# Seven products for the last two token chunks of layer one's first gMLP half

## The chip, the cores and the metric

The kernel runs on one core of a Trainium2 chip. The metric is the device time of one execution, in microseconds (us). A core has five engines with queues of their own: TensorE (PE in the profile; its weight loads are PEld) multiplies, VectorE (DVE) and GpSimd (POOL) do elementwise work, ScalarE (ACT) applies functions and copies, SyncE (SP) starts DMA transfers. GpSimd starts some transfers too. Each engine works through its queue in the order in which the program recorded it, and waits on semaphores for the others.

## The reference

Two layers, each a linear attention block and then a gated MLP, on 2048 tokens of 512 features, all in float32. Each block adds its result to x. The second half of the MLP is normalised and mixed over the tokens by a 2048 x 2048 matrix.

```python
def _B_ref(x, w_in, w_sp, b_sp, w_out):
    z = _gelu(jnp.einsum("bsd,df->bsf", x, w_in))
    z1 = z[..., :Fh]
    z2 = _layernorm(z[..., Fh:], axis=-1)
    g = jnp.einsum("ts,bsf->btf", w_sp, z2) + b_sp[None, :, None]
    return jnp.einsum("bsf,fd->bsd", z1 * g, w_out)
...
x = A_x
x = x + _A_ref(_layernorm(x, axis=-1), A_wqkv, A_wo)
x = x + _B_ref(_layernorm(x, axis=-1), B_w_in, B_w_sp, B_b_sp, B_w_out)
x = x + _A_ref(_layernorm(x, axis=-1), A_wqkv, A_wo)
x = x + _B_ref(_layernorm(x, axis=-1), B_w_in, B_w_sp, B_b_sp, B_w_out)
```

w_in is 512 x 1792, Fh is 896.

## The kernel before

A float32 product is made of three matmuls in a faster type: each operand is split into a high part (`high`, a copy by ScalarE) and a low part (`low`, a subtraction by VectorE), and high x high, low x high and high x low are added up in a PSUM bank (`mm3`, L228 to L230). Tokens go in 16 tiles of 128 (`NT`), or four chunks of 512 (`NCHK`); Fh is seven feature blocks of 128 (`NF`).

The class `P2` is the stage of a layer that ends the attention and makes both halves of the MLP's first product. `run` is layer one's loop over steps s = 1 to 18. In step s, one after another: `b` splits the turned attention result of tile s; `c` multiplies tile s - 1 by the output weights (12 matmuls of 512 columns); `c2` adds it to x and takes the statistics; `c3` normalises the tile (ScalarE) and writes it to memory, from where it is read back to be turned by VectorE (`Turn`: stores by L419, loads by L196, the turn L448); `d` splits the turned tile s - 2 into the operands `xT` of its chunk; `e4` normalises the MLP's second half of tile s - 4 with a mean and a scale (`zms`); `e` multiplies tile s - 3 by the second half's weights (two banks of 448 columns, 24 matmuls), `e2` puts both through gelu, `e3` takes the statistics of the 896 columns, by VectorE in layer one; and twice `f` makes one feature block of the first half, transposed, for a whole chunk (12 matmuls of 512), with gelu and a store (`fout`) behind. So an f can only be made once the four tiles of its chunk are there. The seven f's that are left after step 18, all of chunk 3, are made at the head of the spatial stage (`P4.run`, the loop `while p2.f()`).

Layer two makes the first six features of chunks 2 and 3 otherwise. The features f and f + 3, the two chunks and the two halves of the 512 inner features make 2 x 2 blocks, and seven products of such blocks do for eight: each is 6 matmuls, and sums and differences of blocks are their operands. `first_a` and `first_b` are products 1 and 2, into the bank u, with a copy of u after product 1 into a second bank y; `T1`, `T1split`, `T2` and `raw` make the operands by VectorE and ScalarE; `tail` makes products 5, 6, 7, 3 and 4 and the sums of the results. The weights' sums are made by `FSums` from win1 and kept in memory (`w1sums`): in layer two's first stage, three pairs f by f, with the additions on GpSimd.

Beside this stage run `sums` (sums and differences of blocks of the spatial weights, four additions on GpSimd for two `tick`s, loads and stores by SyncE) and, in steps 9 to 15, the stores of the split weights win1 for layer two (`w1parts`, two a step, `WSTORE`). The last `LEFT` ticks are left to the spatial stage, which is a list of steps g: 14 of the product P2 (12 matmuls of 512 columns each), then P1 with 24 each, and so on (L1922 to L1924).

The order of all queues is that of these calls as written; small tables (`WSTORE`, `WADD`, `LEFT`, `FILL`) say in which step a piece is recorded. Tiles are taken from lists of SBUF pages (pg), quads (qd), bigs (bg), and PSUM banks.

## Time and profile before

| what | value |
|---|---|
| median of 3 runs | 1345.61 us (1345.12 to 1345.69) |
| profiled execution, its own time | 1345.32 us |
| its span | 1343.5 us |
| TensorE busy, share | 1338.9 us, 100% |
| VectorE, ScalarE, GpSimd busy | 1042.9, 726.6, 460.2 us |
| granted TensorE clock | 1.0 |
| layer one's e(11) to the spatial stage | 282.31 to 350.30 us |

The page's groups give line, engine, operation, tiles (out <- in), shape, busy time, mean, and idle time before; the timeline gives start and length of single instructions; lines with SPq or POOL and DMA are the issues of transfers. A matmul's recorded length overlaps its neighbours', so the time from start to start is the one that counts.

### The profile page before, as it was taken

What the parts mean: (1) busy time and instruction counts of PE and PEld (TensorE: products, weight loads), DVE (VectorE), ACT (ScalarE), POOL (GpSimd) and SP (SyncE); (2) the same over time, 40 slices, a digit from 0 to 9 for tenths busy, and PEclk for the clock granted to TensorE, in tenths of its full rate; (3) what the DMA queues carried; (4) which work ended last, traced back from release to release, by engine and by line L of the source; (5) the groups of instructions that cost most, each with busy time, mean ns of one, the idle gap of its engine ahead of it and who ended that gap; (6) DMA issues with size and microseconds to landing.
All of it is one profiled execution on the core that took longest, in us unless ns stands there. A gap on an engine that the chain in (4) does not pass through costs nothing.

```text
span 1343.5 us, 19219 instructions
## 1 busy us (share of the span) xinstructions
PE 1338.9 (100%) x6547; PEld 1142.0 (85%) x6547; DVE 1042.9 (78%) x1662; ACT 726.6 (54%) x1219; POOL 460.2 (34%) x613
## 2 busy tenths in 40 slices
PE   9999999999999999999999999999999999999999
PEld 7888888888888888889988888888888888888898
DVE  7779877753797699898867878777679858899885
ACT  5764634334642265445677755557687433666454
POOL 3755765534122400301425443544531012122021
PEclk9999999999999999999999999999999999999999
DMA  5898477878977986894777662678767545579344
GB/s 184 284 313 282 158 256 250 284 254 270 316 234 256 289 267 203 282 320 80 174 169 235 167 142 84 202 243 259 229 211 234 170 164 176 178 245 312 123 79 64
DMA packets 172403, 290.30 MB, mean 216 GB/s; under 512 B 14480, under 2 KB 53904, under 8 KB 172048
## 3 DMA queue, kind: packets, MB, share of 16 engines
q1 hardware_dynamic: 154048, 251.45, 56.5%
q0 software_dynamic: 18112, 37.49, 13.4%
q8 instruction: 51, 0.84, 0.3%
q14 instruction: 48, 0.39, 0.1%
q10 hardware_dynamic: 144, 0.13, 0.0%
HBM read 204.08 MB, written 101.71 MB: 228 GB/s over the span
## 4 chain that ended last, share of the span: by engine, by line
PE 98%; DVE 1%; DMA 0%; ACT 0%; POOL 0%; issue 0%; SPq 0%; POOLq 0%
PE bank L230 14%; PE bank L228 14%; PE bank L229 14%; PE bank L1922 12%; PE bank L1923 12%; PE bank L1924 12%; PE bank L2120 3%; PE bank L2121 3%; PE bank L2122 3%; PE bank L988 1%; PE bank L989 1%; PE bank L990 1%; PE bank L384 1%; PE bank L1155 1%; PE bank L1157 1%; PE bank L1156 1%
## 5 line engine op out<-in xcount | busy, mean ns | idle before, releaser
L1923 PE MATMUL bank<-qd,pg 128*128 128x512 f32 x736 | 286.4, 389 | 0.0
L1922 PE MATMUL bank<-qd,pg 128*128 128x512 f32 x736 | 286.3, 389 | 0.0
L1924 PE MATMUL bank<-qd,pg 128*128 128x512 f32 x736 | 286.3, 389 | 0.0
L1697 ACT ACTIVATE qd<-qd 128x1024 fp32r<-128x1024 f32 x142 | 149.5, 1053 | 128.2 <-PE bank L1924 108.0
L1700 DVE TENSOR_TENSOR qd<-qd,qd 128x1024 fp32r<-128x1024 f32 x132 | 167.8, 1274 | 54.1 <-ACT qd L1697 54.1
L230 PE MATMUL bank<-qd,pg 128*128 128x512 f32 x448 | 174.7, 390 | 0.0
L1924 PEld LDWEIGHTS bank<-qd,pg 128*128 128x128 f32 x736 | 138.2, 188 | 28.8
L1923 PEld LDWEIGHTS bank<-qd,pg 128*128 128x128 f32 x736 | 138.2, 188 | 28.6
L1922 PEld LDWEIGHTS bank<-qd,pg 128*128 128x128 f32 x736 | 138.2, 188 | 28.6
L1963 POOL TENSOR_TENSOR bg<-bg,pg 128x512 f32<-128x512 f32 x28 | 46.9, 1676 | 217.9 <-ACT qd L1697 100.3
L228 PE MATMUL bank<-qd,pg 128*128 128x512 f32 x308 | 120.2, 390 | 0.2 <-ACT pg L214 0.2
L229 PE MATMUL bank<-qd,pg 128*128 128x512 f32 x308 | 120.0, 390 | 0.0
L230 PEld LDWEIGHTS bank<-qd,pg 128*128 128x128 f32 x448 | 84.1, 188 | 18.2 <-DVE pg L217 0.4
L363 POOL TENSOR_SCALAR rs<-mv 128x1 f32<-128x1 f32 x80 | 24.7, 308 | 191.3 <-DVE mv L361 186.9
L214 ACT ACTIVATE pg<-pg 128x512 fp32r<-128x512 f32 x85 | 53.0, 624 | 64.6 <-DVE pg L448 21.3
L372 ACT ACTIVATE pg<-pg,nb,rs 128x512 f32<-128x512 f32 x52 | 42.1, 812 | 84.5 <-POOL nb L366 79.0
L1606 POOL TENSOR_TENSOR pg<-pg,pg 128x512 f32<-128x512 f32 x48 | 67.2, 1400 | 58.2 <-DVE pg L1762 52.1
L2122 PE MATMUL bank<-wo,qd 128*128 128x256 f32 x288 | 81.5, 283 | 0.0
L2120 PE MATMUL bank<-wo,qd 128*128 128x256 f32 x276 | 78.1, 283 | 0.0
L2121 PE MATMUL bank<-wo,qd 128*128 128x256 f32 x276 | 78.0, 283 | 0.0
L229 PEld LDWEIGHTS bank<-qd,pg 128*128 128x128 f32 x308 | 57.8, 188 | 12.1 <-DVE qd L217 0.3
L228 PEld LDWEIGHTS bank<-qd,pg 128*128 128x128 f32 x308 | 57.8, 188 | 12.1 <-ACT pg L214 0.4
(278 smaller groups left out, 3280.4 us busy)
## 6 DMA issues: line engine op xcount, KB each, us to landing
qd<-s SPq DMA_DIRECT2D x62, 512.0 KB, 4.4
qd<-in_wsp_dram SPq DMA_DIRECT2D x40, 512.0 KB, 4.1
qd<-hP SPq DMA_DIRECT2D x40, 512.0 KB, 4.7
pg<-z SPq DMA_DIRECT2D x56, 256.0 KB, 4.7
pg<-in_wsp_dram SPq DMA_DIRECT2D x52, 256.0 KB, 4.3
s<-pg SPq DMA_DIRECT2D x48, 256.0 KB, 3.8
z<-pg SPq DMA_DIRECT2D x40, 256.0 KB, 3.3
pg<-w POOLq DMA_DIRECT2D x38, 256.0 KB, 4.7
```

Of the source, the lines that this page charges most:

```text
L228: nc.tensor.matmul(out, ah, bh, start=start, stop=False)
L229: nc.tensor.matmul(out, ah, bl, start=False, stop=False)
L230: nc.tensor.matmul(out, al, bh, start=False, stop=stop)
L1606: nc.gpsimd.tensor_tensor(t, a, b, op=OP.add)
L1697: self.mark = nc.scalar.activation(w[:, 0], r, AF.Copy)
L1700: nc.vector.tensor_sub(w[:, 1], r, w[:, 0].bitcast(F32))
L1922: m(out, h[:, o], w[:, 0, j, :], start=start, stop=False, skip_group_check=True)
L1923: m(out, h[:, o], w[:, 1, j, :], start=False, stop=False, skip_group_check=True)
L1924: m(out, l[:, o], w[:, 0, j, :], start=False, stop=stop, skip_group_check=True)
L2120: m(out, A, x, start=start and f == 0, stop=False, skip_group_check=True)
L2121: m(out, A, y, start=False, stop=False, skip_group_check=True)
L2122: m(out, B, x, start=False, stop=stop and f == 2, skip_group_check=True)
```

## The change

Layer one gets the seven products for features 0 to 5 of chunks 2 and 3. `run` records no f of chunk 3 but the seventh, `FONE` says how many f's a step has, product 1 of pair s - 15 stands at the head of steps 15, 16 and 17 with its copy, product 2 at their ends, and `tail` now serves both layers at the head of the spatial stage. Tile 15 is turned by TensorE (four transposes) rather than through memory. The statistics of tiles 10 to 15 are ScalarE's: the gelu's accumulated sum, a square with a sum, and GpSimd's small operations. The weights' sums are loaded, added (now VectorE), split and stored in steps 13 to 18. The w1parts stores move from steps 9 to 15 to steps 4 to 10. Ten ticks of the spatial sums, not four, are left to the spatial stage, from g = 13 on, their loads fetched at g = 12 rather than 14. Turned tiles above 4 lie in the z tiles.

```diff
-WSTORE = 9
+WSTORE = 4
...
-WADD = {2: 0, 4: 1, 6: 2}
+FONE = {6: 2, 7: 2, 8: 2, 9: 1, 10: 2, 11: 2, 12: 2, 13: 1, 14: 1}
+WADD = {13: 0, 14: 1, 15: 2}
...
-LEFT = 4
+LEFT = 10
+TLAST = 13
+TFIRST = 13
+ACTFROM = 10
...
+            self.raw, self.kept, self.made = {}, deque(), []
...
-                nc.gpsimd.tensor_tensor(o, a, b, op=op)
+            self.raw[f] = [load(win1_d[f + 3 * k]) for k in range(2)]
...
+            raw = self.raw.pop(f)
+            p, q = (t.rearrange("p (k n) -> p k n", k=2) for t in raw)
+            V = nc.vector
+            V.tensor_add(q[:, 1], q[:, 0], q[:, 1])
+            V.tensor_sub(q[:, 0], p[:, 0], q[:, 0])
+            V.tensor_sub(p[:, 0], q[:, 1], p[:, 0])
+            V.tensor_sub(p[:, 1], p[:, 1], p[:, 0])
...
+                h, l = pages.get(PAGE, F32R), pages.get(PAGE, F32R)
...
+                self.made.append((f, m, h, l))
+            pages.put(*raw)
+        def store(self):
+            for f, m, *t in self.made:
...
+                    nc.sync.dma_start(w1sums[f, m][k], t[k].bitcast(F32))
+                if m:
+                    pages.put(*t)
+                else:
+                    self.kept.append(t)
+            self.made = []
...
-            self.wf = deque([w1parts[f] for f in list(range(NF)) * 2 + [0, 6, 1, 2, 6]]
+            self.wf = deque([] if not L else [w1parts[f] for f in list(range(NF)) * 2 + [0, 6, 1, 2, 6]]
...
-            self.qturn, self.xturn = Turn(f"qt{L}", range(5), True), Turn(f"yt{L}", (0, 1, 2, 3, NT - 1) if L else range(4), home=ZHome if L else None)
+            self.qturn, self.xturn = Turn(f"qt{L}", range(5), True), Turn(f"yt{L}", (0, 1, 2, 3, NT - 1), home=ZHome, copy=bool(L))
...
+        def by_act(self, i):
+            return self.L or i >= ACTFROM
...
-                more = {"accum_out": self.acc(i)[:, j:j + 1]} if self.L else {}
+                more = {"accum_out": self.acc(i)[:, j:j + 1]} if self.by_act(i) else {}
...
-            if not self.L:
+            if not self.by_act(i):
...
-                w = self.A[f] = self.ws.popleft()
+                w = self.A[f] = self.ws.popleft() if self.L else self.held1(f)
...
-                pages.put(*w)
+                if self.L:
+                    pages.put(*w)
+        def held1(self, f):
+            return [t[:, f].rearrange("p c n -> p (c n)") for t in (self.win1.h, self.win1.l)]
...
-                if f:
+                if f and self.L:
...
+        def tsplit(self, r):
+            if r not in self.T:
+                self.T6q = quads.get([P, 2, 2, 512], F32R)
+                self.T[r] = self.T6q[:, 0], self.T6q[:, 1]
+            t = self.t2 if r == 6 else self.b22
+            for k in range(2):
+                high(self.T[r][0][:, k], t[k])
+            for k in range(2):
+                low(self.T[r][1][:, k], t[k], self.T[r][0][:, k])
...
-            big = [bigs.get([P, NF, 512], F32R if k < 2 else F32) for k in range(3)]
-            c = [big[2][:, f] for f in range(3)]
-            room = Rooms(big[2][:, f] for f in range(3, NF))
+            L = self.L
+            big = [bigs.get([P, NF, 512], F32R if k < 2 else F32) for k in range(3 if L else 2)]
+            if L:
+                c = [big[2][:, f] for f in range(3)]
+                room = Rooms(big[2][:, f] for f in range(3, NF))
+            else:
+                c = [pages.get(PAGE) for _ in range(3)]
+                room = pages
...
-            self.T |= {6: (two(0, 0), two(0, 1)), 7: (two(0, 2), two(1, 0)), 4: (two(1, 1), two(1, 2))}
+            self.T |= {7: (two(0, 2), two(1, 0)), 4: (two(1, 1), two(1, 2))}
+            if L:
+                self.T[6] = two(0, 0), two(0, 1)
+                self.tsplit(6)
+            self.tsplit(7)
...
-            for r, t in ((6, self.t2), (7, self.b22)):
-                for k in range(2):
-                    high(self.T[r][0][:, k], t[k])
-                for k in range(2):
-                    low(self.T[r][1][:, k], t[k], self.T[r][0][:, k])
...
-            self.p4.loadb()
+            if L:
+                self.p4.loadb()
...
-                if f == 0:
+                if L and f == 0:
...
-                if f == 1:
+                if L and f == 1:
...
-            self.e3(NT - 2)
-            self.e3(NT - 1)
-            self.e4(NT - 4)
-            self.e4(NT - 3)
+            if not L:
+                quads.put(self.T6q)
+            if L:
+                self.e3(NT - 2)
+                self.e3(NT - 1)
+                self.e4(NT - 4)
+                self.e4(NT - 3)
...
-            for i in (NT - 2, NT - 1):
+            for i in (NT - 2, NT - 1) if L else ():
...
-                w = self.ws.popleft()
+                w = self.ws.popleft() if L else [t[:, 256:512] for t in self.held1(f + 3)]
...
-                pages.put(*w)
+                if L:
+                    pages.put(*w)
+            if not L:
+                self.win1.free()
...
+            if not L:
+                pages.put(*c)
...
                 return
             w1 = self.win1
             for s in range(1, NT + 3):
-                if s == NT + 2:
-                    sums.tick()
+                if s in (15, 16, 17):
+                    self.first_a(s - 15)
                 self.loadx(s + 1)
                 self.qturn.load(s + 1)
                 if s in self.qturn.by_pe:
...
+                if s == NT + 1:
+                    self.T1()
+                    self.T1split()
+                    self.T2()
+                if s == NT + 2:
+                    self.ws.extend(self.fsums.kept)
+                    quads.put(*self.xT.pop(2))
+                    self.tsplit(6)
+                    for _ in range(3):
+                        self.wfetch()
...
                     self.e(s - 3)
                     self.e2(s - 3)
                     self.e3(s - 3)
-                self.f()
-                self.f()
+                for _ in range(FONE.get(s, 0)):
+                    self.f()
+                if s in (15, 16, 17):
+                    self.first_b(s - 15)
+                    self.first_out(s - 15)
+                if s - 2 in WADD:
+                    self.fsums.store()
+                if s in WADD:
+                    if not WADD[s]:
+                        self.fsums = FSums()
+                    self.fsums.load(WADD[s])
+                if s - 1 in WADD:
+                    self.fsums.split(WADD[s - 1])
+                if s == NT:
+                    self.B = quads.get([P, 2, 2, 512])
+                    self.raw(0)
+                    self.raw(1)
+                    self.wf.extend(w1sums[f, 1] for f in range(3))
                 self.fq.extend(self.fnext)
                 self.fnext = []
                 w1.piece(True)
                 w1.fetch()
                 if self.L == 0:
-                    if s > 4:
-                        sums.tick(s < NT + 2)
+                    if s == TLAST + 1:
+                        sums.store()
+                    if 4 < s <= TLAST:
+                        sums.tick(s < TLAST)
                     if s >= WSTORE and s < WSTORE + NF:
                         for k, t in enumerate((w1.h, w1.l)):
                             nc.sync.dma_start(w1parts[s - WSTORE][k],
                                               t[:, s - WSTORE].rearrange("p c n -> p (c n)").bitcast(F32))
-                if s >= NT + 1:
-                    self.p4.fetch(s - NT - 1)
+                if s == NT + 2:
+                    self.p4.fetch(1)
             self.e4(NT - 1)
             self.win2.free()
...
-            if not early:
-                self.fetch(3)
-                self.sp(0)
-                self.fetch(4)
...
-            if not early:
-                self.zahead(1)
...
-            if early:
-                for _ in p2.tail():
-                    n += 1
-                    self.zahead(n - 1)
-                    self.sp(n - 1)
-                    if n < 3:
-                        self.fetch(n + 3)
-                self.zahead(3)
-            while p2.f():
-                self.zahead(min(self.zmade, 3))
+            for _ in p2.tail():
...
-                if n == SPN:
-                    self.sp(1)
-                    self.fetch(5)
+                self.zahead(n - 1)
+                self.sp(n - 1)
+                if n < 3:
+                    self.fetch(n + 3)
...
-            if p2.win1 is not None:
-                p2.win1.free()
...
-                if not early and g == 14:
+                if not early and g == TFIRST - 1:
...
-                if not early and 15 <= g <= 15 + LEFT:
+                if not early and TFIRST <= g <= TFIRST + LEFT:
...
```

The order, at three places. First ScalarE in the last two steps of the loop and behind it, before: gelus (L1070), outputs (L1137), normalise (L372), then the first split of the spatial stage.

```order
L1070 ACTIVATE z14_z0_3637<-bank5_136_3611 128x448
L1070 ACTIVATE z14_z0_3637<-bank6_137_3624 128x448
L1137 ACTIVATE pg6_368_3663<-bank4_138_3650 128x512
L372 ACTIVATE z14_z0_3637<-z14_z0_3637,nb_3648,rs_3645 128x896
L1070 ACTIVATE z15_z0_3712<-bank7_139_3686 128x448
L1070 ACTIVATE z15_z0_3712<-bank1_140_3699 128x448
L1137 ACTIVATE pg11_373_3738<-bank3_141_3725 128x512
L1137 ACTIVATE pg14_374_3755<-bank0_142_3742 128x512
L372 ACTIVATE z15_z0_3712<-z15_z0_3712,nb_3723,rs_3720 128x896
L1697 ACTIVATE qd4_20_3768<-qd1_18_3677 128x1024
```

And now, from e4(14) on: gelus (L1074), square (L1091), e4(15), two splits for product 7 (L218), the copies of product 5 (L1258), f's output (L1141) and the first copies of product 6 (L1274) into the banks of product 7.

```order
L376 ACTIVATE z14_z0_3648<-z14_z0_3648,acc_3649 128x896
L1074 ACTIVATE z15_z0_3716,acc_3717<-bank4_140_3690 128x448
L1074 ACTIVATE z15_z0_3716,acc_3717<-bank7_141_3703 128x448
L1091 ACTIVATE pg15_356_3721,acc_3717<-z15_z0_3716,acc_3717 128x896
L376 ACTIVATE z15_z0_3716<-z15_z0_3716,acc_3717 128x896
L218 ACTIVATE bg2_7_3730<-pg2_344_3609 128x512
L218 ACTIVATE bg2_7_3730<-pg13_345_3610 128x512
L1258 ACTIVATE pg8_357_3732<-bank5_143_3754 128x512
L1258 ACTIVATE pg6_358_3733<-bank6_144_3762 128x512
L1258 ACTIVATE pg14_359_3734<-bank4_145_3770 128x512
L1141 ACTIVATE pg20_360_3778<-bank2_142_3741 128x512
L1274 ACTIVATE bank5_146_3788<-bank3_125_3359 128x512
```

Between a tile's gelus and its e4 stands the square now, and the two splits and three copies stand behind e4(15).

GpSimd at the same place, now: the last three operations of tile 14 (L1100 to L1102), a store of an output, six loads of the weights' sums (L209), and tile 15's mean (L1081) with its three.

```order
L1100 TENSOR_SCALAR acc<-acc 128x1
L1101 TENSOR_TENSOR acc<-acc,mhalf 128x1
L1102 TENSOR_SCALAR acc<-acc 128x1
L1151 DMA z_0_2_2_3666<-pg_349_3664 128x512
L209 DMA pg_350_3677<-w1s_1_0_111 128x512
L209 DMA pg_351_3679<-w1s_1_1_112 128x512
L209 DMA pg_352_3681<-w1s_1_0_115 128x512
L209 DMA pg_353_3683<-w1s_1_1_116 128x512
L209 DMA pg_354_3685<-w1s_1_0_119 128x512
L209 DMA pg_355_3687<-w1s_1_1_120 128x512
L1081 TENSOR_SCALAR acc<-acc 128x1
```

Before, additions of the spatial sums (L1606) stood between the small operations of two tiles; now seven transfers stand between those of the last two.

VectorE ahead of product 5's operand, only now: the last lows of the weights' sums (L221), the two raw sums of chunk 2 (L1166), the low part of tile 15, and the operand (L1200, L1201, and its low part, L221). Of these, only low(15) stood there before.

```order
L221 TENSOR_TENSOR pg21_341_3574<-pg15_332_3459,pg0_340_3573 128x256
L221 TENSOR_TENSOR pg7_343_3580<-pg8_333_3461,pg20_342_3579 128x256
L221 TENSOR_TENSOR pg7_343_3580<-pg15_332_3459,pg20_342_3579 128x256
L1166 TENSOR_TENSOR qd1_18_3585<-qd4_14_2766,qd5_15_2767 128x1024 x2
L221 TENSOR_TENSOR qd3_17_3278<-bank7_137_3597,qd2_16_3277 128x4x128
L1200 TENSOR_TENSOR qd1_18_3585<-qd2_16_3277,qd1_18_3585 128x1024
L1201 TENSOR_TENSOR qd1_18_3585<-qd1_18_3585,qd3_17_3278 128x1024
L221 TENSOR_TENSOR qd0_19_3606<-qd1_18_3585,qd0_19_3606 128x1024
L1212 TENSOR_TENSOR pg2_344_3609<-qd2_16_3277,qd3_17_3278 128x512
```

Behind them follow the sums and differences of the other products.

SyncE from tile 12's load (yt) to the last load of an attention result (qt), before: an output's store, two stores and three loads of the spatial sums (L1601, in_wsp), two w1parts stores (L1356), a load of x.

```order
L196 DMA pg_334_3168<-yt_12_3161 128x512
L1140 DMA z_0_1_6_3224<-pg_335_3222 128x512
L1601 DMA s_145<-pg_313_2975 128x512
L1601 DMA s_5_134<-pg_312_2973 128x512
L196 DMA pg_336_3228<-in_wsp_dram 128x512
L196 DMA pg_337_3230<-in_wsp_dram 128x512
L196 DMA pg_338_3232<-in_wsp_dram 128x512
L1356 DMA w_4_0_103<-bg_5_1766 128x512
L1356 DMA w_4_1_104<-bg_6_1767 128x512
L196 DMA pg_339_3238<-in_x_dram 128x512
L196 DMA pg_340_3240<-qt_15_3156 128x512
```

And now:

```order
L200 DMA pg_309_3174<-yt_12_3167 128x512
L1144 DMA z_0_1_6_3227<-pg_311_3225 128x512
L200 DMA pg_312_3229<-in_win_dram 128x512
L200 DMA pg_313_3231<-in_win_dram 128x512
L1660 DMA s_145<-pg_294_2985 128x512
L1660 DMA s_5_134<-pg_293_2983 128x512
L200 DMA pg_314_3237<-in_x_dram 128x512
L200 DMA pg_315_3239<-qt_15_3162 128x512
```

Three loads and two stores are gone from between the two loads, and two loads for the weights' sums (in_win) have come.

36 lines of the change are left out of this document (7 added, 29 removed).

## The prediction

> **What bounds the kernel now.** I read the page's busy times first (the first line), then TensorE's waits (the last two lines are all of them, with us in total, times, longest), then the timeline of the stage that is edited.
>
> ```profile
> PE 1338.9 (100%) x6547; PEld 1142.0 (85%) x6547; DVE 1042.9 (78%) x1662; ACT 726.6 (54%) x1219; POOL 460.2 (34%) x613
> PE bank L612 <- DVE ones_f L179: 1.0, 1, 1.0
> PE bank L228 <- ACT pg L214: 0.2, 1, 0.2
> ```
>
> TensorE issues matmuls back to back and waits 1.2 us in all. So a removed matmul is worth its whole pitch, no other engine can give anything back, and every new wait of TensorE is a full loss. The profiled execution took 1345.32 us, 1.8 more than its span of 1343.5; the sum is made against it, and the median of 1345.61 lies 0.3 above.
>
> **What the change removes: 3.65 us.** Timeline of TensorE (start, length): e(11) begins; e(15) begins; the seven last f's of layer one begin; the spatial stage begins; then, from layer two, four transposes and what follows them.
>
> ```profile
> 282.31 0.36 PE L228 MATMUL bank<-bg,qd 128*128 128x448 f32 x1
> 326.36 0.36 PE L228 MATMUL bank<-bg,qd 128*128 128x448 f32 x1
> 331.23 0.39 PE L228 MATMUL bank<-qd,bg 128*128 128x512 f32 x1
> 350.30 0.39 PE L1922 MATMUL bank<-qd,pg 128*128 128x512 f32 x1
> 976.18 0.60 PE L384 MATMUL bank<-ident,z_y 128*128 128x128 f32 x4
> 976.54 0.47 PE L1155 MATMUL bank<-qd,pg 128*128 128x512 f32 x1
> 976.85 0.39 PE L1156 MATMUL bank<-qd,pg 128*128 128x512 f32 x1
> ```
>
> The recorded 0.39 overlaps its neighbours; the pitch is (350.30 - 331.23) / 84 = 0.227. An e is 331.23 - 326.36 = 4.87, a c or an f of 12 matmuls 2.72, half of one 1.36. Three pairs of features in two chunks took 12 x 12 = 144 matmuls and take 3 x 7 x 6 = 126: 18 x 0.227 = 4.09 off. Turning tile 15 on TensorE adds 0.36 to the next start and 0.31 - 0.23 to the one after: 0.44. Net -3.65.
>
> If nothing waits, TensorE's new times follow from e(11), which stays at 282.31: 4.87 + 2.72 end step 14 at 289.9; steps 15 and 16 (half, c, e, half) take 10.3 each, so c(14) ends at 294.0, c(15) at 304.3, e(13) at 309.1; the transposes end at 312.3, e(14) at 317.2, e(15) at 323.4, the last f at 326.1, products 5 and 6 at 330.2 and 334.25. Product 7 is due then, and the spatial stage at 346.5 rather than 350.3.
>
> **What it adds: the wait before product 7, 4.3 us (3.0 to 11).** Product 7 sums into the bank that ScalarE copies out of product 6's, and that copy stands last in an in-order ScalarE queue. Layer two already runs these instructions, so its timeline has their durations: four of VectorE, six of ScalarE, three of GpSimd. Where a piece of the change has no row of its own I take the nearest: 0.55 for a ScalarE copy or output of 512 columns (993.19: four in 2.21), 0.5 for a gelu, 0.25 for a mean on GpSimd (L1096).
>
> ```profile
> 978.21 0.69 DVE L217 TENSOR_TENSOR qd<-z_y,qd 128x512 fp32r<-128x512 f32 x1 [0.70 <-ACT qd L214]
> 982.05 1.22 DVE L1192 TENSOR_TENSOR qd<-qd,qd 128x1024 f32<-128x1024 f32 x1
> 987.84 1.22 DVE L1162 TENSOR_TENSOR qd<-qd,qd 128x1024 f32<-128x1024 f32 x1
> 967.55 0.68 DVE L909 TENSOR_TENSOR pg<-pg,bank 128x512 f32<-128x512 f32 x1
> ...
> 970.58 0.81 ACT L372 ACTIVATE z_y<-pg,nb,rs 128x512 f32<-128x512 f32 x1
> 985.08 1.05 ACT L214 ACTIVATE qd<-qd 128x1024 fp32r<-128x1024 f32 x1
> 986.98 2.17 ACT L372 ACTIVATE z_z<-z_z,acc 128x896 f32<-128x896 f32 x2
> 989.03 0.55 ACT L1007 ACTIVATE z_z<-bank 128x448 f32<-128x448 f32 x1
> 993.19 2.21 ACT L214 ACTIVATE bg<-pg 128x512 fp32r<-128x512 f32 x4
> 1002.93 1.03 ACT L1087 ACTIVATE pg<-z_z,acc 128x896 bf16<-128x896 f32 x1
> 1003.86 0.19 ACT L1087 ACTIVATION_READ_ACCUMULATOR pg<-z_z,acc 128x1 f32 x1
> ...
> 965.58 0.25 POOL L1096 TENSOR_SCALAR acc<-acc 128x1 f32<-128x1 f32 x1
> 966.76 0.29 POOL L1098 TENSOR_SCALAR acc<-acc 128x1 f32<-128x1 f32 x1
> 970.71 2.22 POOL L205 DMA_DIRECT2D pg<-w1s  x4 [0.19 <-issue]
> ```
>
> The chain, along the order of the queues:
> - Tile 15's normalise stands ahead of tile 14's high part on ScalarE. From c(15) at 304.3: add, statistics (967.55 to 970.58 is 3.0) and 0.81 give 308.1; the high part, 0.6, ends at **308.7**.
> - ScalarE: e4(12) 1.1, two gelus 1.0, a mean on GpSimd 0.3, square with its read 1.2, output 0.6, four half-width splits of the weight sums (1.6, below the 2.21 of full width): 314.6.
> - VectorE: the last low of those sums 0.4, two raw sums 2.4, low(15) 0.7, the two operations of product 5's operand 2.45 (twice L1192): 320.6. Only then is there something to split for ScalarE's next instruction; the ScalarE work of e(14), which TensorE ended at 317.2, stands behind it. VectorE's other operands wait there too, but are needed later.
> - ScalarE: split 1.05, e4(13) 1.1, gelus 1.0, mean 0.3, square 1.2: 325.3; output 0.6, two splits 1.1, e4(14) 1.1, gelus(15) 1.0: 329.1.
> - GpSimd: after the three small operations of tile 14 (965.58 to the end of L1098, 1.5: 326.8) stand one store and six loads of the weight sums at 0.55, to 330.7, and tile 15's mean is queued behind them: 331.0. Square 1.2, three operations 1.5, e4(15) 1.1, two splits 1.1, three copies 1.65, an output 0.6, the copy 0.55: **338.6**.
>
> Product 7, due at 334.25, waits 4.3; products 3 and 4 follow it at their pitch, since what they read is split while 7 runs. Where these queues overlap better than I added, some 1.3 could fall away: lower end 3.0, the row of high(14) still deciding. The upper end comes from tile 14's round trip through memory, which I took to be in time. Here are SyncE's issues from the store of tile 12 to the last query load, and the VectorE and ScalarE rows that hang on that load, in the kernel before:
>
> ```profile
> 287.15 0.32 SPq L196 DMA_DIRECT2D pg<-yt  x1
> ...
> 288.98 1.55 SPq L196 DMA_DIRECT2D pg<-in_wsp_dram  x3
> 290.57 0.95 SPq L1356 DMA_DIRECT2D w<-bg  x2
> ...
> 292.13 1.26 SPq L196 DMA_DIRECT2D pg<-qt  x1
> ...
> 289.09 0.67 DVE L909 TENSOR_TENSOR pg<-pg,bank 128x512 f32<-128x512 f32 x1
> 298.81 1.10 DVE L448 STREAM_TRANSPOSE pg<-pg 128x512 f32<-128x512 f32 x1 [2.38 <-DMA pg<-qt]
> 301.22 0.68 DVE L909 TENSOR_TENSOR pg<-pg,bank 128x512 f32<-128x512 f32 x1
> ...
> 314.75 0.62 ACT L214 ACTIVATE qd<-pg 128x512 fp32r<-128x512 f32 x1
> ...
> pg<-z SPq DMA_DIRECT2D x56, 256.0 KB, 4.7
> ```
>
> The load lands 6.7 after its issue, tile 14's add follows 2.4 later, its high part ends at 315.4. TensorE is ahead of this round trip already, by 301.2 less the new 294.0. Kept as it is, the chain from 308.7 starts at 315.4 and product 7 at 345.3, 11 late; e(14) itself, due at 312.3, would have waited 3 of those. But the change takes five of these issues (three loads, two stores: 2.5 us) out and puts two weight loads in, about 0.95: 1.6 sooner, and with less traffic the landing may be nearer to 4.7, the page's median for a load of that size (the last row). I take the round trip as just in time, since the two gains together are some 3.6 of the 6.7 and the rest may come from the missing stores of steps 11 to 13; this is the weakest choice here.
>
> **Edits at no cost.** The stores of the weight parts in steps 4 to 10: 0.95 a step in SyncE's queue ahead of a query load. From the chain of waits before e(7), the only wait of TensorE in this stage:
>
> ```profile
> 216.09 3.66 DMA pg<-qt
> 223.20 1.09 DVE pg L448
> ```
>
> The load lands at 219.75 and VectorE turns it at 223.2: 3.4 of cover. Without it 0.95 would be lost once, and the wait at product 7, which is set by the other engines, would shrink by the same. ScalarE's new statistics in steps 13 to 18 and the sums taken off GpSimd in layer two cost and give nothing beside that chain: TensorE waits for none of the latter now.
>
> **The spatial sums, 0.5 (0 to 1.9).** Their fetch moves two steps of 2.72 ahead, so GpSimd's adds begin at 388.1 rather than 393.58, while VectorE is about to empty the second product's last banks (L1872).
>
> ```profile
> 389.34 1.28 DVE L1872 TENSOR_TENSOR bg<-pg,bank 128x512 f32<-128x512 f32 x2
> 391.67 0.55 DVE L1737 TENSOR_TENSOR z_z<-z_z 128x384 f32<-128x384 f32 x1
> 394.47 1.65 DVE L1737 TENSOR_TENSOR z_z<-z_z 128x384 f32<-128x384 f32 x1
> ...
> 393.58 6.96 POOL L1606 TENSOR_TENSOR pg<-pg,pg 128x512 f32<-128x512 f32 x4 [52.12 <-DVE pg L1762]
> ```
>
> Beside those adds L1737 takes three times its 0.55. Two or three such operations stand ahead of the evacuation, so the end of its first half slides from 390.0 to between 392.2 and 393.3; the seventh unit of the next product needs that bank at 388.4 + 6 x 0.68 = 392.5 (350.30 + 14 steps of 2.72; a unit is three matmuls). I take the middle, 0.5; a fourth operation under the adds makes 1.9.
>
> Sum: 1345.32 - 3.65 + 4.3 + 0.5 = 1346.47, so **1346.5**.
>
> **Rivals.** *All of the saving stays* (0.24): the round trip and both queues keep ahead, 1345.32 - 3.65 = 1341.7, with up to 0.9 of waits left 1342.6. For it speaks that layer two runs the same products with no wait of TensorE; against it that there the last tiles' statistics stand behind the copies, and here ahead of them. *The round trip cannot follow* (0.33): steps of 10.3 rather than 13 us meet a trip that comes 12.1 apart (289.1 to 301.2 for this add in tiles 13 and 14). With the 1.6 of SyncE alone high(14) ends at 313.8, 5.1 behind 308.7, and product 7 waits 9.4: 1345.32 - 3.65 + 9.4 + 0.5 = 1351.6; with 3.6 it is 1349.6. It decides once high(14) ends after 310.5, where the sum passes 1348.3. *A slow restart* (0.08): the trace's first five matmuls of 512 columns take 2.33 (0.47 each); if TensorE came out of a 4.3 us gap like that, five matmuls would add 1.2: 1347.7.
>
> ```profile
> 3.77 2.33 PE L619 MATMUL bank<-pg,ones 128*128 128x512 f32 x5
> ```
>
> [...]
>
> **How the numbers follow.** The forecast has 0.35, between 1343.0 and 1348.3, the slow restart 0.08 beside it. A measurement of this kernel tells about 0.2%, 2.7 us, from no change: faster is below 1342.9, slower above 1348.3. Faster is the first rival, 0.24; slower the second and a little of the restart, 0.35; the rest, 0.41, is within. The range 1342.0 to 1352.0 leaves out 0.05 below and 0.12 above.
>
> **What would show it.** Right: one wait of TensorE of 3 to 5 us ahead of product 7, released by ScalarE's copy out of the bank, six load issues of GpSimd between tile 14's and tile 15's statistics, and ScalarE idle about 5 us ahead of product 5's split. Wrong: no wait over 1 us (1342), or waits at e(13) or e(14) released by the split of z_y, with high(14) after 312. A later e(7) would mean that the early stores are not covered, and a wait at the seventh unit of over 2 us that the sums' price is too low.

## The result

The changed kernel takes 1358.26 us, the median of four executions (1357.19 to 1359.19), against 1345.63 for the kernel before (four executions, 1345.12 to 1345.69). The ratio is 1.0094 with a 95% interval of 1.0077 to 1.0112: 12.6 us slower. (A single execution of the last kernel of the experiments, which took 3368.03 us, is left out.) The forecast was 1346.5, its range ended at 1352.0, and its likeliest outcome was no change that can be told.

The profiled execution of the changed kernel has a span of 1357.4 us, 13.9 more than before. The page's busy times, and the first line of its chain that ended last:

```profile
PE 1340.4 (99%) x6533; PEld 1138.6 (84%) x6533; DVE 1066.3 (79%) x1681; ACT 741.9 (55%) x1258; POOL 467.0 (34%) x621
...
PE 92%; ACT 2%; DVE 2%; DMA 1%; issue 1%; POOL 1%; SPq 0%; ACTq 0%; DVEq 0%; POOLq 0%
```

TensorE's busy time stayed while the span grew by 13.9, so TensorE now waits. These are its waits between 100 and 500 us of the changed kernel (what waited, what released it; us in total, times, longest). In the same stretch the kernel before had none; the two waits that the prediction shows lie before it.

```profile
PE bank L1159 <- ACT bank L1274: 3.8, 1, 3.8
PE bank L232 <- ACT qd L218: 1.9, 2, 1.0
PE bank L232 <- ACT z_z L1074: 1.7, 2, 1.4
PE bank L1159 <- ACT z_z L1074: 1.4, 1, 1.4
PE bank L1159 <- ACT bank L1176: 1.0, 2, 0.5
PE bank L388 <- ACT z_y L376: 0.8, 1, 0.8
PE bank L234 <- DVE qd L221: 0.3, 1, 0.3
```

The first row is product 7, the wait that was forecast at 4.3. All the others were priced at nothing: e(11) and e(13) wait for the high part of their tile (second row), e(14) for a bank that gelu still reads (third), product 5 for the same after e(15) (fourth), the second products in the loop for the copy of the first (fifth), the transposes for tile 15's normalise (sixth), and the third matmul of e(15) for the low part of its tile (last). They sum to 10.9.

TensorE's timeline gives the places: e(11) begins; e(14) begins, after the longest wait inside the loop; e(15) begins; product 7 begins after its wait, and the matmul behind it; the spatial stage begins.

```profile
283.74 0.47 PE L232 MATMUL bank<-bg,qd 128*128 128x448 f32 x1 [0.89 <-ACT qd L218]
...
320.58 0.47 PE L232 MATMUL bank<-bg,qd 128*128 128x448 f32 x1 [1.40 <-ACT z_z L1074]
...
326.93 0.36 PE L232 MATMUL bank<-bg,qd 128*128 128x448 f32 x1
...
349.51 0.80 PE L1159 MATMUL bank<-bg,pg 128*128 128x512 f32 x1 [3.79 <-ACT bank L1274]
350.10 0.63 PE L1160 MATMUL bank<-bg,pg 128*128 128x512 f32 x1
...
363.43 0.39 PE L1981 MATMUL bank<-qd,pg 128*128 128x512 f32 x1
```

| TensorE begins | e(11) | e(12) | e(13) | e(14) | e(15) | product 7 | spatial stage |
|---|---|---|---|---|---|---|---|
| kernel before | 282.31 | 295.36 | 308.42 | 318.75 | 326.36 | - | 350.30 |
| times of the prediction with no wait | 282.31 | 293.97 | 304.3 | 312.3 | 318.5 | 334.25 | 346.5 |
| measured | 283.74 | 296.08 | 308.76 | 320.58 | 326.93 | 349.51 | 363.43 |
| late against no wait | 1.4 | 2.1 | 4.5 | 8.3 | 8.4 | 15.3 | 16.9 |

(The third and fourth entries of the second row are that prediction's steps taken on: in its order e(13) follows c(15), and e(14) the transposes; the prediction's 317.2 and 323.4 are the ends of e(14) and e(15).) Half of the lateness is there by e(15), inside the loop, where no step was priced at anything. The rows above put 5.1 of the 8.4 into waits. Most of the other 3.3 lies around the restarts: from start to start a wait costs more than the idle time recorded for it, since a recorded length (0.39) is longer than the pitch (0.227) and overlaps its neighbour's (at product 7 it is 4.18 from start to start, 3.95 over the pitch, for 3.79 of idle time), and the first matmul behind it is recorded at 0.47 to 0.50 rather than 0.36 to 0.39. From e(15) to product 7 another 6.9 is lost, 5.2 of it in the two waits of products 5 and 7. The last 1.6 is a slow restart. The table by stretch around it (length; busy time and count of TensorE, weight loads, VectorE, ScalarE, GpSimd; granted clock; DMA share; GB/s):

```profile
345.00:350.00 5.00, 1.21 (x5) 0.75 (x4) 3.01 (x5) 5.00 (x10) 0.00 (x0) 0.94 0.14 46
350.00:352.40 2.40, 2.40 (x7) 1.82 (x7) 2.36 (x4) 2.40 (x5) 0.00 (x0) 0.50 0.82 277
```

The clock is 0.50 behind the gap. Another 0.6 is lost behind the start of the spatial stage. Together 16.9 + 0.6 = 17.5 of loss, less the 3.65 that was removed, make 13.9, the span's growth.

**What replaced TensorE as the limit.** Between these two tiles the chain of waits of the changed kernel doesn't pass through TensorE. One round of it, from the high part of one tile to that of the next (start, length, what):

```profile
308.10 0.61 ACT qd L218
308.71 1.02 ACT z_z L376
309.73 1.05 ACT z_z L1074 x4
...
312.45 0.48 ACT pg L1149
312.93 0.31 ACT pg L218
...
313.32 1.43 DVE pg L221 x4
314.75 0.61 DVE pg L909
315.38 0.70 DVE st L363
...
317.35 0.28 POOL nb L370
...
318.37 0.61 ACT qd L218
```

This round takes 10.27 us (308.10 to 318.37), the one ahead of it 12.69 (from 295.41). The tile itself is VectorE's add, its statistics, GpSimd's small operations, ScalarE's normalise and high part; ahead of them, in the same in-order queues, stand the normalise, the gelus and the square of earlier tiles, and then ScalarE's and VectorE's splits of the weights' sums (0.31 and 1.43 on this chain). TensorE, whose steps with no wait are 10.3 and, from e(13) to e(14), 8.0, can only follow.

The kernel before stood at a second limit too, but at another one, and at its last tile. The rows of VectorE that turn tile 15 and make its low part, there:

```profile
323.71 1.09 DVE L448 STREAM_TRANSPOSE pg<-pg 128x512 f32<-128x512 f32 x1 [5.39 <-DMA pg<-yt]
...
325.50 0.69 DVE L217 TENSOR_TENSOR qd<-pg,qd 128x512 fp32r<-128x512 f32 x1 [0.70 <-ACT qd L214]
```

VectorE waits 5.39 for tile 15 to come back from memory. The low part ends at 326.19, and TensorE began e(15) at 326.36; its third matmul reads that part. TensorE never waited there, yet a TensorE more than 0.6 earlier would have (worked out from these rows). The changed kernel turns tile 15 on TensorE, so this trip through memory is gone from it. Its low part of tile 15 ends at 327.74, 1.55 later, and stands behind VectorE's lows and raw sums of the new products.

The work behind the last tile has grown as well. The spatial stage began 23.9 us after e(15) before the change. Now, with no wait, the same stretch would be 346.5 - 318.5 = 28.0, since the products 5, 6, 7, 3 and 4 stand behind the last tile and the loop lost two f's for two halves a step.

### The profile page after: what moved, and what is told of

The parts are those of the page before. It is cut to its first block, busy times and chain, and to the rows that moved or that the text cites. A ratio compares the mean times of both kernels' runs of the same rounds, so it can differ in the third digit from the quotient of the medians.

```text
span 1357.4 us, 19249 instructions
## 1 busy us (share of the span) xinstructions
PE 1340.4 (99%) x6533; PEld 1138.6 (84%) x6533; DVE 1066.3 (79%) x1681; ACT 741.9 (55%) x1258; POOL 467.0 (34%) x621
## 4 chain that ended last, share of the span: by engine, by line
PE 92%; ACT 2%; DVE 2%; DMA 1%; issue 1%; POOL 1%; SPq 0%; ACTq 0%; DVEq 0%; POOLq 0%
PE bank L1981 12%; PE bank L1982 12%; PE bank L1983 12%; PE bank L232 12%; PE bank L233 12%; PE bank L234 12%; PE bank L2179 3%; PE bank L2180 3%; PE bank L2181 3%; PE bank L988 1%; PE bank L989 1%; PE bank L990 1%; PE bank L1159 1%; PE bank L1160 1%; PE bank L1161 1%
## 5 line engine op out<-in xcount | busy, mean ns | idle before, releaser
L1981 PE MATMUL bank<-qd,pg 128*128 128x512 f32 x736 | 286.4, 389 | 0.0
L1983 PE MATMUL bank<-qd,pg 128*128 128x512 f32 x736 | 286.4, 389 | 0.0
L1982 PE MATMUL bank<-qd,pg 128*128 128x512 f32 x736 | 286.3, 389 | 0.0
L234 PE MATMUL bank<-qd,pg 128*128 128x512 f32 x448 | 174.8, 390 | 0.0
L1983 PEld LDWEIGHTS bank<-qd,pg 128*128 128x128 f32 x736 | 138.2, 188 | 29.0 <-DVE pg L1821 0.3
L1981 PEld LDWEIGHTS bank<-qd,pg 128*128 128x128 f32 x736 | 138.2, 188 | 28.9 <-ACT pg L1819 0.3
L1982 PEld LDWEIGHTS bank<-qd,pg 128*128 128x128 f32 x736 | 138.2, 188 | 28.5
L2022 POOL TENSOR_TENSOR bg<-bg,pg 128x512 f32<-128x512 f32 x28 | 50.5, 1806 | 189.5 <-ACT qd L1756 95.3
L232 PE MATMUL bank<-qd,pg 128*128 128x512 f32 x264 | 103.3, 391 | 0.9 <-DVE pg L221 0.7
L233 PE MATMUL bank<-qd,pg 128*128 128x512 f32 x264 | 103.0, 390 | 0.0
L234 PEld LDWEIGHTS bank<-qd,pg 128*128 128x128 f32 x448 | 84.1, 188 | 18.4 <-DVE pg L221 0.7
L1665 POOL TENSOR_TENSOR pg<-pg,pg 128x512 f32<-128x512 f32 x48 | 70.5, 1469 | 59.1 <-DVE bg L1931 42.2
L218 ACT ACTIVATE pg<-pg 128x512 fp32r<-128x512 f32 (+1 forms) x86 | 49.9, 592 | 40.3 <-DVE pg L1850 19.5
L232 PE MATMUL bank<-bg,qd 128*128 128x448 f32 x160 | 59.4, 371 | 3.3 <-ACT qd L218 1.9
L221 DVE TENSOR_TENSOR pg<-pg,pg 128x512 fp32r<-128x512 f32 (+1 forms) x84 | 54.4, 657 | 9.8 <-ACT pg L218 8.9
L547 POOL TENSOR_TENSOR pg<-pg,pg 128x512 f32<-128x512 f32 x30 | 39.9, 1330 | 57.9 <-DVE pg L541 56.0
```

Of the source, the lines that this page charges most:

```text
L232: nc.tensor.matmul(out, ah, bh, start=start, stop=False)
L233: nc.tensor.matmul(out, ah, bl, start=False, stop=False)
L234: nc.tensor.matmul(out, al, bh, start=False, stop=stop)
L1665: nc.gpsimd.tensor_tensor(t, a, b, op=OP.add)
L1981: m(out, h[:, o], w[:, 0, j, :], start=start, stop=False, skip_group_check=True)
L1982: m(out, h[:, o], w[:, 1, j, :], start=False, stop=False, skip_group_check=True)
```

## The experiments

Two theories stood against each other. A: the loop is bound by the chain from tile to tile as much as by TensorE, so work taken out of the loop is worth nothing, and work put behind the last tile counts in full. B: the saving counts wherever it is made, and it was eaten by new work in the queues (stores, sums, statistics) that could be moved away. Each comparison is with the kernel before on the same chip (medians 1346.28, 1345.49 and 1345.78 in the three sessions); the changed kernel stands at 1358.26.

### Leave 18 matmuls out: inside the loop, and behind the last tile

```diff
-                mm3(b, (wh, wl), (h[:, c, :], l[:, c, :]), c == 0, c == 3)
+                if self.L or n != 2 or f > 5 or c < 3:
+                    mm3(b, (wh, wl), (h[:, c, :], l[:, c, :]), c == 0, c == (2 if not self.L and n == 2 and f < 6 else 3))
```

The first kernel does this to the kernel before for chunk 2, whose f's run in the loop, the second (`n == 3`) for chunk 3, whose f's run behind the last tile. Either removes 4.09 us of TensorE's work.

> The kernel before, with 18 matmuls of 512 columns left out where the change saves them: the last three matmuls of each of the six f's of chunk 2 that stand in steps 14 to 16 (so z1 of that chunk is not the reference's). Theory A, the tiles' round trip through ScalarE, VectorE and memory ends the loop, and those f's only filled TensorE's time beside it: TensorE then waits at e(13), e(14) or e(15), the gain is 0 to 1.5 us of the 4.1, 1344.1 to 1345.6. Theory B, TensorE's own work ends the loop, as its 1.2 us of waits seem to say: the whole 4.1, 1341.5.

> The same 18 matmuls left out of the six f's of chunk 3, which stand behind the last tile (z1 of that chunk is not the reference's). Both theories: no tile is awaited there, so the whole 18 x 0.227 = 4.1 us, 1341.5. If it is much less, the start of the spatial stage waits for something else, and A is not the whole.

In the loop: 1345.93, ratio 0.9996 (0.9983 to 1.0010), no change. Behind the last tile: 1341.41, ratio 0.9966 (0.9954 to 0.9977), 4.6 to 4.9 us faster, the whole work. TensorE's waits of the first kernel in the loop:

```profile
PE bank L228 <- ACT qd L214: 3.7, 2, 3.3
```

From its timeline, e(15), VectorE's turn of tile 15, and the ScalarE row that released e(15):

```profile
327.65 0.49 PE L228 MATMUL bank<-bg,qd 128*128 128x448 f32 x1 [3.25 <-ACT qd L214]
...
325.85 1.08 DVE L448 STREAM_TRANSPOSE pg<-pg 128x512 f32<-128x512 f32 x1 [6.74 <-DMA pg<-yt]
...
326.96 0.63 ACT L214 ACTIVATE qd<-pg 128x512 fp32r<-128x512 f32 x1 [7.95 <-DVE pg L448]
```

TensorE waited 3.3 at e(15) for tile 15's high part, which hangs on the turn, and the turn on the tile's load from memory. (Executions of this kernel spread from 1343.27 to 1349.81, and the profiled one is the longest: its high part begins at 326.96, 2.1 later than in the kernel before, and its clock was granted at 0.93 between 329 and 345 us, behind the wait. Four of the ten lie between 1343.27 and 1343.96, so in some a part of the saving comes through.) In the second kernel the largest new wait is 0.5, in the spatial stage. For the kernel before theory A holds: the same 18 matmuls are worth nothing that can be told at one place (by the interval at most 2.3 of their 4.09) and all of their time at another. For the loop of the changed kernel the test says little, since the trip on which e(15) waits here is the one that the change does away with. That loop is tested by the runs without the early stores and without the sums, below.

### The stores of the weight parts, back in steps 9 to 15, and moved alone

```diff
-WSTORE = 4
+WSTORE = 9
```

> The changed kernel with the stores of the weight parts back in steps 9 to 15. If the early stores made tile 10 late (its low part ends 2.3 us later than before, and e(11) waits 1.3 us): the wait at e(11) goes, and the time falls by 1 to 2.3, to 1356 to 1357. If they are covered, as the prediction had it: no wait is less, within 0.7 of 1358.3, or slower, since the stores come back among the weight sums' own.

> The kernel before with one part of the change alone: the stores of the weight parts in steps 4 to 10. As the prediction had it (3.4 us of cover ahead of the turn): no change, within 0.5 us. If they make the tiles late: a wait of 1 to 3 at e(7) or e(11), and that much slower, 1346.5 to 1348.5.

The changed kernel with the old place: 1354.97, ratio 1.0064 (1.0049 to 1.0079), 3.3 below the changed kernel. The kernel before with the new place alone: 1349.93, ratio 1.0029 (1.0017 to 1.0040), 4.1 slower than before. Both sides agree that these stores cost 3 to 4. In the first kernel the waits of e(11), e(13), the second products and e(15)'s low part are gone, and those behind the loop's first three e's stay: 3.8 at product 7, 1.7 and 1.4 for the banks that gelu reads, 0.7 at the transposes. Its e(11), e(12) and e(13) begin at 282.32, 294.01 and 304.34, the times of no wait to within 0.1. So steps of 10.3 us were possible up to there, and the 4.5 us by which e(13) was late in the changed kernel went with these stores. The wait at e(11) doesn't come with every kernel that has them early: in two of those below (the statistics undone, and the loads recorded later) e(11) begins at 281.88 and 281.75, in time, and only e(13) is late, by about 2. The whole times of those runs differ by this wait too. Why the stores cost is seen between 235 and 286 us. First the waits, of VectorE for the store of a tile that is turned through memory, in the kernel before:

```profile
DVE pg L448 <- DMA yt<-pg: 5.0, 3, 2.8
```

The same, and TensorE's wait at e(11), with the stores in steps 4 to 10:

```profile
DVE pg L448 <- DMA yt<-pg: 8.5, 3, 3.8
...
PE bank L228 <- ACT qd L214: 1.5, 1, 1.5
```

Then the DMA view of that stretch (size, median us from issue to landing of those stores), in the kernel before:

```profile
yt<-pg SPq DMA_DIRECT2D x4, 256.0 KB, 5.0
```

and with the early stores:

```profile
yt<-pg SPq DMA_DIRECT2D x4, 256.0 KB, 5.7
```

The tile's store (yt) takes 0.7 longer to land, VectorE waits 3.5 more for it in three waits, and TensorE 1.5 at e(11). (This execution, 1348.17, is the fastest of seven, so the rows show a part of the 4.1 only.) In the changed kernel it is the load of the query tiles (qt) for which VectorE waits. In the same stretch, with the early stores and with the stores back:

```profile
DVE pg L453 <- DMA pg<-qt: 10.7, 4, 3.0
...
DVE pg L453 <- DMA pg<-qt: 3.8, 2, 3.3
```

The prediction read a cover of 3.4 at one such load, ahead of e(7). By tile 14 VectorE already waited 2.38 for the same kind of load in the kernel before, in a row that the prediction itself shows.

### ScalarE's statistics, undone and alone

```diff
-ACTFROM = 10
+ACTFROM = 16
```

The second kernel puts the statistics of tiles 10 to 15 on ScalarE in the kernel before, and nothing else.

> The changed kernel with the statistics of tiles 10 to 15 by VectorE again. If ScalarE's in-order queue sets the pace of the last rounds (from one tile's high part to the next 12.7 and 10.3 us, in which a mean on GpSimd, the square and its read stand, some 2.3): 4 to 7 us faster, 1351 to 1354, with less wait at e(12) to e(14), and a shorter wait at product 7. If VectorE is as late: no gain or 1 to 2 slower.

> The kernel before with the statistics of tiles 10 to 15 by ScalarE and GpSimd alone. As the prediction had it (costs nothing beside the chain at product 7): no change, within 0.5 us. If a mean, a square and its read (2.3 us) in ScalarE's queue lengthen each round: waits at e(12) to e(15), 1 to 4 us slower.

Undone in the changed kernel: 1357.11, ratio 1.0084 (1.0067 to 1.0101), whose interval overlaps that of the changed kernel: no gain that can be told, as the second of the two expectations had it; the 4 to 7 of the first didn't come. Alone in the kernel before: 1345.78, ratio 1.0000 (0.9990 to 1.0009). The statistics cost nothing that can be told at either place. In the first of the two the wait changed its place:

```profile
PE bank L1159 <- ACT z_z L1074: 3.8, 1, 3.8
...
PE bank L1159 <- ACT bank L1274: 0.8, 1, 0.8
```

Product 7 waits 0.8 rather than 3.8, and product 5's bank 3.8 rather than 1.4. The same ScalarE work, gelu(15) ahead of the copies, seems to be late at whichever of the two comes first.

### The queues in front of product 7

The first kernel records the six loads of the weights' sums behind tile 15's statistics; the second records the making of product 5's operands behind e, e2 and e3 of step 17, so that ScalarE's gelus don't stand behind their split.

```diff
-                    for _ in range(3):
-                        self.wfetch()
...
                     self.e3(s - 3)
+                if s == NT + 2:
+                    for _ in range(3):
+                        self.wfetch()
```

```diff
-                if s == NT + 1:
-                    self.T1()
-                    self.T1split()
-                    self.T2()
...
                     self.e3(s - 3)
+                if s == NT + 1:
+                    self.T1()
+                    self.T1split()
+                    self.T2()
```

> The changed kernel with GpSimd's six loads of the weight sums recorded behind tile 15's statistics, not ahead of them. If those six issues (3.3 us in the trace) are what the chain to product 7 waits for: the wait of 3.8 falls to about 0.5, and the slow matmuls behind it (1.8) go too, 5 us faster, 1353. If ScalarE's own queue is as late, or the loads are then missed by product 7 instead: 0 to 1.5 faster, 1357 to 1358.

> The changed kernel with the operands of products 5 to 7 (T1, its split, T2) recorded behind tile 14's gelus and square in step 17. If ScalarE's idle of 4.8 us ahead of product 5's split is what makes the tail late: gelus and square of tile 14 come some 5 us sooner, the waits at product 6 (1.6) and product 7 (3.8) and the slow matmuls (1.8) go, 5 to 7 us faster, 1351 to 1353. If GpSimd's loads alone set the tail: product 7 waits as long as now, 1357 to 1358.

The loads: 1355.41, ratio 1.0073 (1.0057 to 1.0088), 2.9 better than the changed kernel. The operands: 1353.43, ratio 1.0059 (1.0042 to 1.0077), 4.8 better (two executions at 1351.6 and 1351.7, two at 1355.1 and 1356.0). In the first, product 7 waits 2.3 instead of 3.8 (0.5 was expected, a miss). In the second it waits 1.8 and product 5's wait is gone. The whole times mislead here, since both edits work near the end of the loop and behind it. From e(15) to the spatial stage the changed kernel takes 36.5, the first of these 34.7 and the second 30.1: gains of 1.8 and 6.4. The first gained the rest ahead of e(15), where its execution had no wait at e(11); in the second's profiled execution TensorE waited 1.9 at e(11) and began e(15) 2.9 later than in the changed kernel. In its own stage the second comes out as expected, so far as one execution can show. The rows of the changed kernel that these two edits undo, from ScalarE's, VectorE's and GpSimd's timelines:

```profile
324.74 0.58 ACT L218 ACTIVATE qd<-bank 128x512 fp32r<-128x512 f32 x1
330.16 1.06 ACT L218 ACTIVATE qd<-qd 128x1024 fp32r<-128x1024 f32 x1 [4.84 <-DVE qd L1201]
...
328.90 1.23 DVE L1201 TENSOR_TENSOR qd<-qd,qd 128x1024 f32<-128x1024 f32 x1
...
338.19 0.64 POOL L1151 DMA_DIRECT2D z<-pg  x1
338.83 3.19 POOL L209 DMA_DIRECT2D pg<-w1s  x6
342.06 0.27 POOL L1081 TENSOR_SCALAR acc<-acc 128x1 f32<-128x1 f32 x1
```

ScalarE stands idle for 4.84 ahead of product 5's split, until VectorE's L1201 ends at 330.13; and tile 15's mean (L1081) stands behind a store and six load issues of GpSimd, 3.8 together. The two places were foretold row by row. Their effects overlap, since either of them alone leaves the other in the same chain.

### No sums of the weights at all

The loads, additions, splits and stores of steps 13 to 18 are left out, and products that need sums get plain parts of the weights instead; TensorE's instructions stay the same in number and shape.

```diff
-                if s - 2 in WADD:
-                    self.fsums.store()
-                if s in WADD:
-                    if not WADD[s]:
-                        self.fsums = FSums()
-                    self.fsums.load(WADD[s])
-                if s - 1 in WADD:
-                    self.fsums.split(WADD[s - 1])
...
-                    self.ws.extend(self.fsums.kept)
+                    self.ws.extend(self.held1(f) for f in range(3))
...
-                    self.wf.extend(w1sums[f, 1] for f in range(3))
+                    self.wf.extend(w1parts[f] for f in range(3))
```

> The changed kernel without the weight sums (not loaded, added, split or stored; the products take weight parts as they are, so z1 of chunks 2 and 3 is not the reference's in both layers). If their splits on ScalarE and VectorE (some 3.3 us a round in steps 14 to 16) lengthen the rounds: the waits at e(12) to e(14) fall from 6.6 by 3 to 6, the tail's waits by a few more, 1349 to 1354. If the rounds are set by the tiles alone: within 1 of 1358.3.

1349.91, ratio 1.0033 (1.0021 to 1.0045), 8.4 below the changed kernel. TensorE's waits:

```profile
PE bank L1159 <- ACT bank L1275: 2.6, 1, 2.6
PE bank L232 <- ACT qd L218: 1.7, 1, 1.7
```

A stretch of the table by windows, inside e(11), behind the second of these waits (columns as above):

```profile
286.50:289.40 2.90, 2.90 (x9) 2.58 (x8) 1.10 (x1) 1.84 (x6) 1.24 (x4) 0.50 0.96 317
```

From e(12) to e(15) TensorE waits no more. It takes 24.6 for this, against 24.5 in the times of no wait and 31.0 in the kernel before, and the rounds from one tile's high part to the next are 10.1 and 7.7 rather than 12.7 and 10.3. So what delayed TensorE there were the sums' pieces in VectorE's, ScalarE's and the DMA queues between two tiles, and the shorter steps count in full once those are gone. The wait at e(11) stays, since the stores are still in steps 4 to 10; with the slow stretch behind it e(12) begins 4.4 late. Product 7 still waits 2.6, and from e(15) to the spatial stage it takes 32.3 where no wait has 28.0. By these two losses this kernel is slower than the one before even without the sums, which are work that the method can't do without.

### The repairs together, and the sums made early

The first kernel takes the stores back to steps 9 to 15, makes product 5's operands late, and records the statistics of tile 15 and the normalising of tiles 14 and 15 behind product 4's splits in `tail`. The second also makes the weights' sums in layer one's first stage, with the additions on GpSimd, and fetches all six pairs in step 18. The third also has `ACTFROM = 16`.

```diff
+                self.e3(NT - 1)
+                self.e4(NT - 2)
+                self.e4(NT - 1)
...
-WADD = {13: 0, 14: 1, 15: 2}
+WADD = {2: 0, 4: 1, 6: 2}
```

> The changed kernel with three orders put right at once: stores of the weight parts in steps 9 to 15, the operands behind tile 14's square, and tile 15's square and the last two e4 recorded in the tail behind product 4's split. From the 1355.0 of the first alone the waits at products 6 and 7 (1.6 and 3.9) and the slow matmuls behind (1.8) should go: 1347 to 1348, still short of the kernel before by the waits at the transposes and e(14) and their slow matmuls (0.9, 1.6, 1.4). If it comes out under 1345, the round trip is no bound once the orders are right.

> a_best with the weight sums made in layer one's first stage, steps 2 to 8, additions on GpSimd, as layer two's first stage had them, and all six pairs fetched in step 18. The waits at the transposes and at e(14) and their slow matmuls (3.9 us) go with the splits out of the rounds: 4 us faster than a_best, about 1345, level with the kernel before. If layer one's first stage has no room for them, TensorE waits there and it stays at 1349 or more.

> a_best2 with the statistics of tiles 10 to 15 by VectorE. If ScalarE's queue still sets the last rounds, 1 to 2 us faster than a_best2, 1343 to 1344, below the kernel before; if VectorE is now the later of the two, as much slower.

The first: 1350.02, ratio 1.0027 (1.0015 to 1.0038), 8.2 below the changed kernel, but slower than the 1347 to 1348 expected and than the kernel before. Products 5 to 7 no longer wait; what waits is e(14) on gelu's bank, as in the changed kernel, and now two units of the spatial stage, it seems on what was pushed back (a second product waits another 0.5):

```profile
PE bank L232 <- ACT z_z L1074: 1.4, 1, 1.4
PE bank L1984 <- DVE bg L2042: 1.2, 1, 1.2
PE bank L388 <- ACT z_y L376: 0.8, 1, 0.8
PE bank L1984 <- ACT pg L1822: 0.7, 1, 0.7
```

Its spatial stage begins at 351.86, 5.4 after the time of no wait and 1.6 after that of the kernel before; another 3.1 is lost behind it. The second and third miss: 1360.64, ratio 1.0103 (1.0088 to 1.0118), and 1364.30, ratio 1.0131 (1.0114 to 1.0148). In the second, the late loop is nearly clean (0.4 at e(14), 1.3 and 0.5 in product 5), but the first stage, between 40 and 140 us, pays for it. TensorE's waits there, and VectorE's for the trip of its tiles through memory (xt), which was 1.9 in the kernel before:

```profile
PE bank L232 <- DVE pg L221: 9.4, 6, 3.5
...
DVE bank L453 <- DMA pg<-xt: 10.0, 4, 3.0
```

This is the same kind of loss as that of the stores, in a stage that also had no wait of TensorE to begin with. No version of the change that was run beats the kernel before.

Read by stage, in the profiled executions, the picture is another one than by the whole times:

| TensorE's time from | e(11) to e(15) | e(15) to the spatial stage |
|---|---|---|
| kernel before | 44.1 | 23.9 |
| times with no wait | 36.2 | 28.0 |
| changed kernel | 43.2 | 36.5 |
| first of these repairs | 41.9 | 28.0 |
| second, sums made early | 37.0 | 30.7 |
| third, statistics by VectorE too | 36.3 | 30.2 |

The third's loop and the first's tail run as with no wait. Over both stages the second takes 67.7 and the third 66.5, where the kernel before has 68.0; they lose elsewhere, at e(11), which begins 14.2 and 15.5 later than before, and the third also in the spatial stage. So each half has run once without loss; 36.3 and 28.0 would make 64.3, 3.7 below the 68.0. No run has both halves and a place for the sums that costs less than that, so whether the method can pay here isn't shown.

## Why the prediction was wrong

- **"I take the round trip as just in time", priced at 0.** This is the step that failed. From e(11) to e(15) TensorE was to take 36.2 and took 43.2, and by e(15) it was 8.4 late. There are two causes, measured apart: without the early stores e(13) was in time and e(15) 4.2 late, and without the sums only the wait at e(11) was left. The prediction's own sign of being wrong came: e(13) waited 0.99 for its high part, and high(14) ended at 318.98, long after 312. The trip itself could follow at 10.1 and 7.7 a round, so the rival that doubted this (0.33, 1349.6 to 1351.6) had the right kind of loss and the wrong reason. It was also too small: it let the delay flow into product 7's wait, while in the run the loss in the loop and the loss at product 7 came one after the other.
- **The basis, "a removed matmul is worth its whole pitch".** Half right, and not what made the miss. It followed from TensorE waiting for 1.2 us in all. The count of matmuls was right (18, 4.09) and so is their worth behind the last tile (4.6 to 4.9 measured). Inside the loop of the kernel before the worth is 0.4 us, with an interval that includes none: a wait of zero says that TensorE is a bound, and not that it is the only one. The margin could have been read from the rows of before, where tile 15's low part ends 0.17 us before e(15). But the trip behind that row is gone from the changed kernel, and without the sums its steps took 24.6 where 24.5 was due.
- **"Edits at no cost": the stores.** Wrong: 4.1 alone, 3.3 when undone. The cover was read at one load of a query tile, and the later one shown, of tile 14, had none; in the kernel before VectorE waited for the store of the normalised tile as well. The sign that the prediction had named, a later e(7), says nothing: e(7) began at 233.20 rather than 232.43, within the scatter of the kernels with late stores (232.18 to 233.33). The wait came at e(11).
- **The sums of the weights.** Wrong by omission: the four splits and the last low part were counted once, on the way to product 7, and not at the other tiles between which they stand. Taken out, they give 8.4 back, about half of it by e(15) and half behind.
- **The wait before product 7, 4.3.** Right: 3.8 measured, and 1.4 more one step earlier at product 5's bank. Both causes are there as written: ScalarE idle for 4.84 (about 5 was said) and six load issues between the statistics of tiles 14 and 15. From the end of high(14) to product 7 the forecast has 29.9 (308.7 to 338.6) and the run 30.5 (318.98 to 349.51). The chain began 10.3 later than forecast, and TensorE came to product 7 11.3 later, so that the difference of the two came out almost as forecast is in part luck.
- **ScalarE's statistics at no cost.** Right: 1.0000 alone, and no difference that can be told when undone.
- **The spatial sums, 0.5.** No wait of TensorE is there between 375 and 400 us in the changed kernel, so 0, inside the range of 0 to 1.9.
- **The slow restart (0.08).** Right and given too small a chance: 1.6 lost behind the gap of 3.8, where 1.2 was worked out from the trace's first five matmuls. Those took 0.47 each at a granted clock of 1.00; behind the gap the clock was 0.50 from 349.45 to 352.80, and the first two matmuls are recorded at 0.80 and 0.63.
- **The sum.** 1345.3 - 3.65 + 4.3 + 0.5 was forecast. With the same terms the run has -3.65, then +8.4 in the loop, +6.9 from e(15) to product 7, +1.6 for the restart, and 0.6 behind. The +8.4 was priced at 0 and is two thirds of the miss.

What stays open: the causes overlap, so that their single gains (3.3, 8.4, 2.9 and 4.8) add up to more than the 12.6. How the 8.4 that the sums cost divides among VectorE, ScalarE and the DMA queues wasn't tried, and why the wait at e(11) comes in some kernels with the early stores and not in others isn't known.

## What to carry to other kernels

An engine that never waits may stand exactly on a second limit (here 18 matmuls left out gave 0.4 us inside the loop and 4.6 to 4.9 behind its last tile): before a saving on it is priced, leave out the same number of instructions at that place and, beside it, at a place behind the last dependence, and see whether the time moves. Then ask whether the limit so found is one that the change itself removes. In a loop where each tile makes a round trip through other engines or through memory, read the cover of every hop (the store, the landing, the load, each engine's queue) before something is put beside it; a few small operations between two tiles in an in-order queue are paid for tile after tile, once the loop hangs on that queue (here rounds of 12.7 and 10.3 us with the pieces of the sums, 10.1 and 7.7 without). Where a loop is bound by such a chain, a method that saves work in it and adds some behind its last tile is priced by what it adds (here 28.0 us with no wait from e(15) to the spatial stage, where 23.9 stood before). And when an edit works in one stage, compare that stage's time as well as the whole: here a wait elsewhere, which came and went, was of the size of what was sought.

## What the runs showed of the hardware

The granted clock fell to 0.50 behind some waits of TensorE and not behind others. It did so behind the 3.8 wait of the changed kernel, for 3.35 us (349.45 to 352.80), and also behind a single wait of 1.7 (the stretch from 286.5 shown above), and behind waits of 0.7 and 1.4 within 4 us, in the changed kernel with its stores back:

```profile
315.90:317.70 1.80, 1.80 (x6) 1.59 (x5) 0.41 (x1) 1.50 (x3) 0.61 (x2) 0.50 1.05 405
```

In the run without the sums the slow stretch began 1.9 us after TensorE was busy again (e(11) begins at 284.62, and from the matmul at 286.48 on the recorded length is 0.55 to 0.57 rather than 0.37). There e(11) took 6.9 rather than 4.87, so the slow stretch and the restart cost 2.0, more than the wait of 1.7 itself. Yet no such stretch came behind the wait of 1.5 at e(11) in the kernel before with early stores (the clock was 1.00 from 285.2 to 289.0), nor behind 2.3 at product 7 in the kernel with its loads later (1.00 from 345 to 354), nor behind the waits of 0.8 and 1.4 in the changed kernel itself (1.00 from 318 to 330). A length from which it happens can't be read from these runs; in one of them a wait of 1.7 in TensorE cost 3.7 with what came behind it.
